# Attention and MLP layer on one core: the maxima's parts and the inverse of the sums move to GpSimd, with one store and two loads of the maxima per tile

## The chip, the cores and the metric

The kernel runs on one core of a Trainium2 chip. Its time is the device time of one execution in microseconds (us), and the time of a kernel is the median of several executions. The engines are named as the profile names them: PE is TensorE's matmul, PEld its weight load, DVE is VectorE, ACT is ScalarE, POOL is GpSimd, and SP is SyncE, which here only issues DMAs. Each engine works through its own instructions in the order in which the program lists them; an instruction that waits holds up all that stand behind it on its engine.

## The reference

The input is one sequence of 2048 rows of 512 numbers. It is normalised, and then goes through two branches whose results are added to the input (S = 2048, D = 512, H = 32 heads of Dh = 16, F = 1792; `q`, `k` and `v` come from `x @ wqkv`):

```python
def _A_ref(x, wqkv, wo):
    ...
    scores = jnp.einsum("bhqd,bhkd->bhqk", q, k) * (Dh ** -0.5)
    p = _softmax(scores, axis=-1)
    o = jnp.einsum("bhqk,bhkd->bhqd", p, v)
    return (lambda x, *d: x.transpose(*d))(o, 0, 2, 1, 3).reshape(B, S, D) @ wo

def _B_ref(x, w1, b1, w2, b2):
    h = jnp.einsum("bsd,df->bsf", x, w1) + b1
    h = _gelu(h)
    return jnp.einsum("bsf,fd->bsd", h, w2) + b2

x = A_x
xn = _layernorm(x, axis=-1)
return x + _A_ref(xn, A_wqkv, A_wo) + _B_ref(xn, B_w1, B_b1, B_w2, B_b2)
```

## The kernel before

**Tiles and units.** The attention is cut into 32 tiles: eight groups of four heads, times four blocks of 512 queries. A tile has 16 units. The function `unit` (from L766) runs once per unit and does two things at once, 19 units apart (`LEAD`). For the tile that is ahead it computes *scores by query*: a product `pS` of 128 queries with 512 keys for each of four heads, of which DVE takes the maximum over the 512 keys (L366, tile `mt`). For the tile 19 units behind it computes *scores by key*: a product `pT` of 128 keys with 512 queries for each of four heads, whose exponential ACT writes to `pe` (L414); the products `pV` of `pe` with the values accumulate over the tile's 16 units. Each product is four matmuls of 32 columns, and works in the upper or the lower 64 rows of PE.

**The filler.** Everything else that PE has to do (projections, both layers of the MLP, the output projection) is cut into products `pD` that `unit` deals out: a group of them has a pace, so that a unit carries 32 or 24 of these matmuls in its two halves (`FAST` and `SLOW`).

**The order inside a unit.** A unit has two halves. In the first it issues `pT`, `pS`, `pS`, `pT` for two of the four heads, and then `pV` and `pD`; in the second the same for the other two heads. Only three PSUM banks hold `pS` (tag S), three hold `pT` (tag T), taken in turn.

**The maxima.** Softmax needs each query's maximum over all keys before the exponential. The maximum, divided by 1024 and negated, is held as two float16 rows (a high part and the rest) in rows 62 and 63 of the operand `qst`, against rows of 1024 in `kst`; the product `pT` then has the maximum subtracted already. So after the last unit of scores of a tile, this chain must be through before `pT` of that tile can start, three units later:

- `s_end` (L375): DVE reduces `mt` to 16 columns of negated maxima, `mneg` (L382), in float32.
- `store` (L385): after the first half of the next unit, PE turns `mneg` with two float32 products against the identity (L390), into a bank of tag T, or of tag S where a group of filler products has just begun (`fresh`).
- DVE writes from that bank the high part (L393) and the rest (L394) into `mhl`.
- SP issues two stores of `mhl` to DRAM (L397) and, when they have landed, four loads into `qst` (L348).

**The sums.** The last column of the values is 1, so `pV` also holds the sums of the exponentials. At the end of a tile (`v_end`, L430) ACT copies `pV` to `osb`; the sums go to DRAM, come back as `dn`, 64x32, DVE inverts them (L458), and they go to DRAM and come back spread over the rows as `rb`. POOL multiplies and splits (L471 to L473). These steps are put into a queue with a delay in units each, 1, 3, 6, 7, 9 and 12 (L483).

**POOL's work** (GELU's products, splits in two float16 parts) is dealt out too: `run_steps` gives out up to `POOL_NS` = 2500 ns of it per unit.

**The start.** The first 19 units of scores, with layernorm and the first projections, are put in order by a planner (`Plan`), which takes the step with the longest chain behind it; `E_TAIL` is the length that it counts behind the first tile's loads of maxima. There the chain of the maxima is written out a second time (L1130 to L1152).

Of the kernel before, what the change touches and what calls it, by code (L numbers as in the profile page):

```python
# [18 lines left out]
P = 128  # L19
# [15 lines left out]
POOL_NS = 2500  # L35
TAIL = 5
WARM = 430
NV = 11
LAG, E_TAIL = 3000, 8000
# [15 lines left out]
def layer_kernel(ctx: ExitStack, tc: tile.TileContext, x, wqkv, wo, w1, b1, w2, b2, out):  # L55
# [19 lines left out]
    m_d = dram.tile([NG * NQB, 16, 2, P], F16, name="m_d")  # L75
# [21 lines left out]
    mnegs = [const.tile([P, 32], F32, name=f"mneg{i}") for i in range(2)]  # L97
    for m in mnegs:
        nc.gpsimd.memset(m, 0.0)
# [244 lines left out]
    def m_rows(t, h):  # L344
        g, qb = divmod(t, NQB)
        p, a = divmod(h, 2)
        dst = qst[g % 2][qb][64 * a + 62:64 * a + 64, p].rearrange("r (t q) -> r t q", q=P)
        nc.sync.dma_start(dst, m_d[t, 4 * h:4 * h + 4].rearrange("t r q -> r t q"))  # L348

    def s_mm(u, n, s):  # L350

        t, i = divmod(u, 16)
        g, qb = divmod(t, NQB)
        qt, kb = divmod(i, 4) if t else (i % 4, i // 4)
        ks, qs = kst[g % 2], qst[g % 2]
        p, a = divmod(n, 2)
        r = slice(64 * a, 64 * a + 62)
        tiled(None, s, qs[qb][r, p, qt * P:(qt + 1) * P], ks[kb][r, p, :], True, True)

    def s_max(u, n, s):  # L360

        t, i = divmod(u, 16)
        qt, kb = divmod(i, 4) if t else (i % 4, i // 4)
        if t not in mt_of:
            mt_of[t] = work.tile([P, 4, 4, 4], F32, name="mt", bufs=2)
        nc.vector.reduce_max(mt_of[t][:, n, qt, kb:kb + 1], s, axis=AX.X)  # L366
        given("dve", 600)
# [7 lines left out]
    def s_end(u):  # L375
# [4 lines left out]
        g, qb = divmod(t, NQB)  # L380
        mneg = mnegs[t % 2]
        nc.vector.tensor_reduce(mneg[:, :16], mt_of[t].rearrange("p h t k -> p (h t) k"), axis=AX.X, op=ALU.max, negate=True)  # L382
        given("dve", 220)

        def store():  # L385
# [3 lines left out]
            for a in range(2):  # L389
                nc.tensor.matmul(pt[32 * a:32 * a + 32, :64], mneg[64 * a:64 * a + 64, :],  # L390
                                 ident[64 * a:64 * a + 64, 64 * a:64 * a + 64], start=True, stop=True)
            mhl = work.tile([64, 2, 64], F16, name="mhl", bufs=2)
            nc.vector.tensor_scalar_mul(mhl[:, 0], pt[:64, :64], 1.0 / MROW)  # L393
            nc.vector.scalar_tensor_tensor(mhl[:, 1], pt[:64, :64], 1.0 / MROW, mhl[:, 0], op0=ALU.mult, op1=ALU.subtract)  # L394
# [35 lines left out]
    def v_end(u):  # L430
# [16 lines left out]
        dn = work.tile([64, 32], F32, name="dn", bufs=1)  # L447
        rb = work.tile([P, QB], F32, name="rb", bufs=1)
# [8 lines left out]
        def inverse():  # L457
            nc.vector.reciprocal(dn, dn)  # L458
            given("dve", 330)
# [23 lines left out]
        at = (1, 3, 6, 7, 9, 12) if t < (NG - 1) * NQB else (1, 2, 5, 6, 7, 8)  # L483
# [282 lines left out]
    def unit(gen):  # L766
# [7 lines left out]
        for a in range(2):  # L774
            for kind, b in ((1, 1), (0, 0), (0, 1), (1, 0)) if a == 0 else ((1, 2), (0, 3), (0, 2), (1, 3)):
# [30 lines left out]
            if a == 0 and u % 16 == 0 and u // 16 - 1 in stores:  # L806
                stores.pop(u // 16 - 1)()
# [12 lines left out]
    with ExitStack() as st1:  # L820
# [309 lines left out]
        def maxima():  # L1130
            nc.vector.tensor_reduce(mnegs[0][:, :16], mt_of[0].rearrange("p h t k -> p (h t) k"), axis=AX.X, op=ALU.max, negate=True)

        a = add("DVE", 220, maxima, m_last)
        mkey = ("S", "m", 0)
        mhl = work.tile([64, 2, 64], F16, name="mhl", bufs=2)

        def turn_m():
            tl[mkey] = sb_tile(mkey)
            for k in range(2):
                nc.tensor.matmul(tl[mkey][32 * k:32 * k + 32, :64], mnegs[0][64 * k:64 * k + 64, :],  # L1140
                                 ident[64 * k:64 * k + 64, 64 * k:64 * k + 64], start=True, stop=True)

        a = add("PE", 300, turn_m, [a], take=[mkey])
        a = add("DVE", 160, lambda: nc.vector.tensor_scalar_mul(mhl[:, 0], tl[mkey][:64, :64], 1.0 / MROW), [a])
        a = add("DVE", 160, lambda: nc.vector.scalar_tensor_tensor(mhl[:, 1], tl[mkey][:64, :64], 1.0 / MROW, mhl[:, 0],
                                                                   op0=ALU.mult, op1=ALU.subtract), [a], free=[mkey])
        put = [add("SP", 600, lambda k=k: nc.sync.dma_start(m_d[0, :, :, 64 * k:64 * k + 64], mhl[32 * k:32 * k + 16]), [a], size=4)
               for k in range(2)]
        for k in range(4):
            def fn(k=k):  # L1150
                m_rows(0, k)
            add("SP", 270, fn, put, size=4, tail=E_TAIL)  # L1152
# [365 lines left out]
```

## Time and profile before

| what | value |
|---|---|
| median of 3 runs | 1451.87 us (1451.73 to 1453.36) |
| the profiled execution's own time | 1450.86 us |
| its span, first to last instruction | 1449.1 us |
| mean granted TensorE clock | 0.996 |
| PE busy | 1432.0 us, 99% of the span |
| DVE busy | 1353.8 us, 93% |
| ACT busy | 1255.9 us, 87% |
| POOL busy | 663.8 us, 46% |
| DMA | 124.86 MB, mean 86 GB/s |

The span is what the profile can account for; 1.8 us of the execution lie around it. Busy time is the union of an engine's instructions: matmuls overlap, so a PE that is always busy can still be late. Rows of a timeline give the start and the length in us, the engine, the line of the kernel, the operation, what it writes and reads, and in brackets the idle time before it with what ended it. Rows of the groups give the count, the busy time of all, the mean in ns of one, and the idle time of the engine just before them. Rows of windows give for each engine the busy time in that stretch, with the number of its instructions.

### The profile page before, as it was taken

Reading aid. Unit: us, or ns where it says so; the run is one execution under the profiler, and the core shown is the slowest. Engines: PE = TensorE matmul, PEld = TensorE weight load, DVE = VectorE, ACT = ScalarE, POOL = GpSimd, SP = SyncE. Lnnn points to the kernel's source line nnn. Section 1 sums busy time; section 2 is a strip of 40 time slices with the busy share of each in tenths; the row PEclk is TensorE's granted clock in tenths of the full one; section 3 lists DMA queues with packets and bytes.
Section 4 is the critical chain, followed back from the end, with each engine's and each line's share of the span. In section 5 each row is a group of like instructions: output and inputs, shape, how many; then the busy total and the mean of one; then the engine's idle time right before and its main releaser. Section 6 shows DMA issues by size and latency. Waiting matters only on the chain.

```text
span 1449.1 us, 88687 instructions
## 1 busy us (share of the span) xinstructions
PE 1432.0 (99%) x40184; PEld 964.6 (67%) x40184; DVE 1353.8 (93%) x2304; ACT 1255.9 (87%) x2367; POOL 663.8 (46%) x673
## 2 busy tenths in 40 slices
PE   8999999999999999999999999999999999999998
PEld 4447767776666767667677766676766767666565
DVE  7989999999999999999999999999999999999933
ACT  5868888888999888899988899998889999888885
POOL 3201857664878401388831138882115787121100
PEclk9999999999999999999999999999999999999999
DMA  7731565455224210221112111121112110111423
GB/s 218 226 122 40 163 202 182 150 181 153 86 64 131 67 34 27 62 70 42 45 44 89 30 37 46 55 74 45 44 39 85 48 38 23 56 55 47 137 65 119
DMA packets 112627, 124.86 MB, mean 86 GB/s; under 512 B 22908, under 2 KB 84220, under 8 KB 112248
## 3 DMA queue, kind: packets, MB, share of 16 engines
q1 hardware_dynamic: 112248, 119.18, 26.8%
q8 instruction: 314, 5.14, 1.5%
q14 instruction: 65, 0.53, 0.1%
HBM read 81.66 MB, written 37.34 MB: 82 GB/s over the span
## 4 chain that ended last, share of the span: by engine, by line
PE 87%; DVE 8%; DMA 2%; ACT 1%; issue 1%; SPq 0%; DVEq 0%; ACTq 0%
PE pD L169 26%; PE pV L169 25%; PE pT L169 17%; PE pS L169 16%; DVE mt L366 7%; PE pT L1015 2%; DMA wq<-in_A_wqkv_dram 1%; PE pD L1015 1%; DMA m_d<-mhl 0%; ACT xs L968 0%; DVE xt L998 0%; ACT pe L414 0%; DMA qst<-m_d 0%; DVE ac L1393 0%; ACT wqk_h L904 0%
## 5 line engine op out<-in xcount | busy, mean ns | idle before, releaser
L366 DVE TENSOR_REDUCE mt<-pS 128x1 f32<-128x512 f32 x2029 | 1277.4, 682 | 34.8 <-PE pS L169 7.8
L414 ACT ACTIVATE pe<-pT 128x512 f32<-128x512 f32 x2048 | 1106.9, 599 | 150.2 <-PE pT L169 65.0
L169 PE MATMUL pV<-pe,vv 64*32 64x512 f32 x8192 | 1087.8, 591 | 0.3 <-issue 0.2
L169 PE MATMUL pT<-qst,kst 64*32 64x512 f16 x8192 | 710.4, 378 | 1.9 <-issue 1.2
L169 PE MATMUL pS<-kst,qst 62*32 62x512 f16 x8116 | 627.0, 378 | 2.6 <-DVE mt L366 2.0
L169 PEld LDWEIGHTS <-qst 62*32 62x32 f16 x8192 | 309.3, 90 | 196.7 <-issue 50.9
L169 PE MATMUL pD<-xb,wc 64*32 64x512 f16 x5376 | 363.9, 375 | 0.0
L169 PE MATMUL pD<-w_s,g 64*32 64x512 f16 x5376 | 361.8, 375 | 0.0
L169 PEld LDWEIGHTS <-kst 64*32 64x32 f16 x8192 | 280.5, 91 | 96.0 <-issue 24.2
L169 PEld LDWEIGHTS pV<-pe,vv 64*32 64x32 f32 x8192 | 245.3, 105 | 13.6 <-PE pV L169 4.2
L169 PEld LDWEIGHTS <-wc 64*32 64x32 f16 x5376 | 160.7, 91 | 44.5 <-issue 0.4
L169 PEld LDWEIGHTS <-g 64*32 64x32 f16 x5376 | 163.5, 91 | 39.2 <-issue 0.5
L169 PE MATMUL pD<-xt,wqk_h 64*32 64x512 f16 x2400 | 159.3, 376 | 0.7 <-issue 0.7
L1360 POOL TENSOR_TENSOR xa<-xa,yt 128x512 f32<-128x512 f32 x16 | 20.5, 1281 | 222.8 <-ACT yt L1358 222.8
L471 POOL TENSOR_TENSOR osb<-osb,rb 128x512 f32<-128x512 f32 x31 | 39.9, 1286 | 159.2 <-DMA rb<-den_d 132.8
L1312 POOL TENSOR_TENSOR t<-hh 128x512 f32<-128x512 f32 x56 | 58.2, 1040 | 77.0 <-ACT hh L1335 75.9
L169 PEld LDWEIGHTS <-wqk_h 64*32 64x32 f16 x2400 | 74.0, 92 | 19.9 <-issue 2.0
L1314 POOL TENSOR_TENSOR t<-t,hh 128x512 f32<-128x512 f32 x56 | 71.8, 1282 | 4.7
L1307 POOL TENSOR_TENSOR t<-t,hh 128x512 f32<-128x512 f32 x56 | 71.7, 1280 | 4.7
L1309 POOL TENSOR_TENSOR g<-t,g 128x512 f16<-128x512 f32 x56 | 65.2, 1164 | 4.7
L1306 POOL TENSOR_SCALAR t<-t,gs 128x512 f32<-128x512 f32 x56 | 38.8, 694 | 54.8 <-ACT t L1301 54.8
L169 PE MATMUL pD<-wo_s,oc 64*32 64x512 f16 x816 | 54.7, 376 | 0.0
(165 smaller groups left out, 895.1 us busy)
## 6 DMA issues: line engine op xcount, KB each, us to landing
wc<-w_d SPq DMA_DIRECT2D x56, 256.0 KB
qk_d<-stg SPq DMA_DIRECT2D x32, 256.0 KB
rb<-den_d SPq DMA_DIRECT2D x124, 64.0 KB
wch<-in_B_w_dram SPq DMA_DIRECT2D x14, 512.0 KB
wch<-in_B_w_dram SPq DMA_DIRECT2D x28, 256.0 KB
w_d<-wsp SPq DMA_DIRECT2D x28, 256.0 KB
kst<-qk_d SPq DMA_DIRECT2D x64, 96.0 KB
qst<-qk_d SPq DMA_DIRECT2D x64, 96.0 KB
```

The source lines that it names most:

```text
L169: p = nc.tensor.matmul(*args, **kw)
L366: nc.vector.reduce_max(mt_of[t][:, n, qt, kb:kb + 1], s, axis=AX.X)
L414: nc.scalar.activation(pe, st, AF.Exp, scale=scale_of[g // 2])
L471: pooled((1280, lambda: nc.gpsimd.tensor_tensor(osb, osb, rb, op=ALU.mult)), (620, lambda: nc.gpsimd.tensor_scalar(ot[:, 0], osb, 1.0, 0.0 ...
L1015: nc.tensor.matmul(tl[key], lhs, rhs, start=c + n == 0, stop=(c, n) == (NC - 1, 2))
L1306: pooled((690, lambda: nc.gpsimd.tensor_scalar(t1, t1, 1.0, gs[:, 1:2], op0=ALU.add, op1=ALU.mult)), (1280, lambda: nc.gpsimd.tensor_tenso ...
L1307: (1280, lambda: nc.gpsimd.tensor_tensor(t1, t1, hh, op=ALU.mult)),
L1309: (1160, lambda: nc.gpsimd.tensor_tensor(g[:, 1, f, :], t1, g[:, 0, f, :], op=ALU.subtract)),
L1312: pooled((1040, lambda: nc.gpsimd.tensor_tensor(t1, hh, hh, op=ALU.mult)), (620, lambda: nc.gpsimd.tensor_scalar(t1, t1, 1.0, 1.0 / GELU_A ...
L1314: (1280, lambda: nc.gpsimd.tensor_tensor(t1, t1, hh, op=ALU.mult)),
L1360: add = lambda: nc.gpsimd.tensor_tensor(xa, xa, yt, op=ALU.add)
```

## The change

What it does:

- DVE still reduces `mt` to 16 columns (now `mx`, not negated). POOL then divides it by 1024, makes the float16 high part, and the float16 rest: three instructions on 128x16 (`m_parts`). DVE's two instructions on the turned maxima are gone.
- PE turns the float16 parts with two products against a float16 matrix of -1 on the diagonal (`m_turn`), and ACT copies the result to `mturned` (`m_copy`). The turning products are issued later: no longer after the first half of the unit, but in the second half, just before its last `pT`.
- `mturned` goes to DRAM in one store, and comes back in two loads. The queries of a block are dealt to the partitions of `pS` in another order (64 from the block's first half, 64 from its second), so that these loads find longer runs; the number of matmuls of `pS` stays.
- The inverse of the sums is four POOL instructions on 64x32: a power with exponent -1, and a Newton step. It is queued with a delay of 5 units (4 for the last group), not 6 (5).
- `POOL_AT`: in the units around the end of a tile `run_steps` gives out 800 ns (before the tile's last unit) and 3100 ns (in the three that follow) of POOL's other work in place of 2500.
- In the start, the planner has the same chain in its new form, and `E_TAIL` is 9500 in place of 8000.

```diff
+POOL_AT = {15: 800, 0: 3100, 1: 3100, 2: 3100}
-LAG, E_TAIL = 3000, 8000
+LAG, E_TAIL = 3000, 9500
-    m_d = dram.tile([NG * NQB, 16, 2, P], F16, name="m_d")
+    m_d = dram.tile([NG * NQB, 2, 2, 2, 8, P // 2], F16, name="m_d")
...
-        room[0] = min(room[0], 0) + POOL_NS
+        room[0] = min(room[0], 0) + (POOL_AT.get(pos[0] % 16, POOL_NS) if pos[0] < NU else POOL_NS)
...
-    def m_rows(t, h):
+    def m_store(t, turned):
+        nc.sync.dma_start(m_d[t].rearrange("s a j r q -> (s a j r) q"), turned)
+
+    def m_rows(t, a):
         g, qb = divmod(t, NQB)
-        p, a = divmod(h, 2)
-        dst = qst[g % 2][qb][64 * a + 62:64 * a + 64, p].rearrange("r (t q) -> r t q", q=P)
-        nc.sync.dma_start(dst, m_d[t, 4 * h:4 * h + 4].rearrange("t r q -> r t q"))
+        dst = qst[g % 2][qb][64 * a + 62:64 * a + 64].rearrange("j p (s n) -> j p s n", s=2)
+        nc.sync.dma_start(dst, m_d[t, :, a].rearrange("s j (p t) q -> j p s (t q)", p=2))
+
+    def m_parts(t):
+        mx = work.tile([P, 2, 8], F32, name="mx", bufs=1)
+        parts = work.tile([P, 2, 2, 8], F16, name="mparts", bufs=2)
+        return (lambda: nc.vector.tensor_reduce(mx.rearrange("p a r -> p (a r)"), mt_of[t].rearrange("p h t k -> p (h t) k"),
+                                                axis=AX.X, op=ALU.max),
+                lambda: nc.gpsimd.tensor_scalar(mx, mx, 1.0 / MROW, 0.0, op0=ALU.mult, op1=ALU.add),
+                lambda: nc.gpsimd.tensor_scalar(parts[:, :, 0], mx, 1.0, 0.0, op0=ALU.mult, op1=ALU.add),
+                lambda: nc.gpsimd.tensor_tensor(parts[:, :, 1], mx, parts[:, :, 0], op=ALU.subtract)), parts
+
+    def m_turn(pt, parts):
+        for s in range(2):
+            nc.tensor.matmul(pt[32 * s:32 * s + 32, :64], parts[64 * s:64 * s + 64].rearrange("p a j r -> p (a j r)"),
+                             nident[64 * s:64 * s + 64], start=True, stop=True)
+
+    def m_copy(pt):
+        turned = work.tile([64, 64], F16, name="mturned", bufs=2)
+        nc.scalar.activation(turned, pt[:64, :64], AF.Copy)
+        return turned
...
-        tiled(None, s, qs[qb][r, p, qt * P:(qt + 1) * P], ks[kb][r, p, :], True, True)
+        for j in range(0, P, 32):
+            c = QB // 2 * (j // 64) + 64 * qt + j % 64
+            product(None, s[j:j + 32], qs[qb][r, p, c:c + 32], ks[kb][r, p, :], start=True, stop=True)
...
-            for a in range(2):
-                nc.tensor.matmul(pt[32 * a:32 * a + 32, :64], mneg[64 * a:64 * a + 64, :],
-                                 ident[64 * a:64 * a + 64, 64 * a:64 * a + 64], start=True, stop=True)
-            mhl = work.tile([64, 2, 64], F16, name="mhl", bufs=2)
-            nc.vector.tensor_scalar_mul(mhl[:, 0], pt[:64, :64], 1.0 / MROW)
-            nc.vector.scalar_tensor_tensor(mhl[:, 1], pt[:64, :64], 1.0 / MROW, mhl[:, 0], op0=ALU.mult, op1=ALU.subtract)
-            given("dve", 300)
-            for a in range(2):
-                nc.sync.dma_start(m_d[t, :, :, 64 * a:64 * a + 64], mhl[32 * a:32 * a + 16])
-            for h in range(4):
-                m_rows(t, h)
+            m_turn(pt, parts)
+            m_store(t, m_copy(pt))
+            for a in (1, 0):
+                m_rows(t, a)
...
         def inverse():
-            nc.vector.reciprocal(dn, dn)
-            given("dve", 330)
+            nc.gpsimd.tensor_tensor(iv, dn, minus1, op=ALU.pow)
+            nc.gpsimd.tensor_tensor(dn, dn, iv, op=ALU.mult)
+            nc.gpsimd.tensor_scalar(dn, dn, -1.0, 2.0, op0=ALU.mult, op1=ALU.add)
+            nc.gpsimd.tensor_tensor(dn, dn, iv, op=ALU.mult)
...
-        at = (1, 3, 6, 7, 9, 12) if t < (NG - 1) * NQB else (1, 2, 5, 6, 7, 8)
+        at = (1, 3, 5, 7, 9, 12) if t < (NG - 1) * NQB else (1, 2, 4, 6, 7, 8)
...
-            for kind, b in ((1, 1), (0, 0), (0, 1), (1, 0)) if a == 0 else ((1, 2), (0, 3), (0, 2), (1, 3)):
+            for i, (kind, b) in enumerate(((1, 1), (0, 0), (0, 1), (1, 0)) if a == 0 else ((1, 2), (0, 3), (0, 2), (1, 3))):
+                if a == 1 and i == 3 and u % 16 == 0 and u // 16 - 1 in stores:
+                    stores.pop(u // 16 - 1)()
...
-            if a == 0 and u % 16 == 0 and u // 16 - 1 in stores:
-                stores.pop(u // 16 - 1)()
```

How this moves instructions is seen best on PE, in the unit that follows a tile's last unit of scores (a tile in the middle of the program, `w_s` and `g` are operands of filler products, `kst` and `qst` the operands of the scores). Before, the turning products stand behind the first half's filler and ahead of the second half's four products of scores:

```order
L169 LDWEIGHTS g
L169 MATMUL pD<-w_s,g 32x512
L390 MATMUL pT<-ident,mneg_100 32x64 x2
L169 LDWEIGHTS kst_3_86
L169 MATMUL pT<-qst_1_92,kst_3_86 32x512
...
L169 LDWEIGHTS qst_3_94
L169 MATMUL pS<-kst_0_83,qst_3_94 32x512
```

Now, in the same unit (`mparts` is what POOL wrote):

```order
L175 LDWEIGHTS g
L175 MATMUL pD<-w_s,g 32x512
L175 LDWEIGHTS kst_3_86
L175 MATMUL pT<-qst_1_92,kst_3_86 32x512
...
L175 LDWEIGHTS qst_3_94
L175 MATMUL pS<-kst_0_83,qst_3_94 32x512
...
L370 LDWEIGHTS mparts
L370 MATMUL pT<-nident,mparts 32x64
...
L175 LDWEIGHTS kst_3_86
L175 MATMUL pT<-qst_1_92,kst_3_86 32x512
```

One `pT` and two `pS` now come ahead of the turning products, and one `pT` behind them.

On POOL, the same kind of place while the MLP's first layer runs: before (`t` and `g` are GELU's tiles, `osb`, `rb` and `ot` the end of the sums' path of the tile before),

```order
L1309 TENSOR_TENSOR g<-t_12832,g 128x512
L1312 TENSOR_TENSOR t_13482<-hh 128x512
L1313 TENSOR_SCALAR t_13482<-t_13482 128x512
L1314 TENSOR_TENSOR t_13482<-t_13482,hh 128x512
L471 TENSOR_TENSOR osb<-osb,rb 128x512
L472 TENSOR_SCALAR ot<-osb 128x512
```

and now:

```order
L1327 TENSOR_TENSOR g<-t_12866,g 128x512
L364 TENSOR_SCALAR mx<-mx 128x16
L365 TENSOR_SCALAR mparts<-mx 128x2x8
L366 TENSOR_TENSOR mparts<-mx,mparts 128x2x8
L1330 TENSOR_TENSOR t_13524<-hh 128x512
L1331 TENSOR_SCALAR t_13524<-t_13524 128x512
L1332 TENSOR_TENSOR t_13524<-t_13524,hh 128x512
L497 TENSOR_TENSOR osb<-osb,rb 128x512
```

The three steps on the maxima stand where POOL's share of a unit has been cut to 800 ns; GELU's next three and the end of the sums' path follow them.

More of the change, by code (lines that the diff above doesn't have):

```diff
@@ L95, in layer_kernel @@
     sexp = const.tile([P, 4], F32, name="sexp")
-    mnegs = [const.tile([P, 32], F32, name=f"mneg{i}") for i in range(2)]
-    for m in mnegs:
-        nc.gpsimd.memset(m, 0.0)
+    nident = const.tile([P, P // 2], F16, name="nident")
+    for a in range(2):
+        nc.gpsimd.tensor_scalar(nident[64 * a:64 * a + 64], ident[64 * a:64 * a + 64, 64 * a:64 * a + 64], -1.0, 0.0,
+                                op0=ALU.mult, op1=ALU.add)
+    minus1 = const.tile([64, 32], F32, name="minus1")
+    nc.gpsimd.memset(minus1, -1.0)
     free_banks = {"S": [0, 1, 2], "T": [3, 4, 5], "D": [6], "V": [7]}
@@ L447, in v_end @@
         dn = work.tile([64, 32], F32, name="dn", bufs=1)
+        iv = work.tile([64, 32], F32, name="iv", bufs=1)
         rb = work.tile([P, QB], F32, name="rb", bufs=1)
@@ L1128, in layer_kernel @@
             score(u)
[L1130 to L1135, printed above, removed]
+        mkey, m_of = ("S", "m", 0), []
+        m_steps, m0 = m_parts(0)
+        a = add("DVE", 220, m_steps[0], m_last)
+        for step in m_steps[1:]:
+            a = add("POOL", 220, step, [a])
         def turn_m():
             tl[mkey] = sb_tile(mkey)
-            for k in range(2):
-                nc.tensor.matmul(tl[mkey][32 * k:32 * k + 32, :64], mnegs[0][64 * k:64 * k + 64, :],
-                                 ident[64 * k:64 * k + 64, 64 * k:64 * k + 64], start=True, stop=True)
+            m_turn(tl[mkey], m0)
         a = add("PE", 300, turn_m, [a], take=[mkey])
[L1144 to L1152, printed above, removed]
+        a = add("ACT", 220, lambda: m_of.append(m_copy(tl[mkey])), [a], free=[mkey])
+        put = add("SP", 420, lambda: m_store(0, m_of[0]), [a], size=4)
+        for k in (1, 0):
+            add("SP", 270, lambda k=k: m_rows(0, k), [put], size=4, tail=E_TAIL)
         for t in range(NV):
```

8 lines of the change are left out of this document (4 added, 4 removed).

## The prediction

> **What bounds the kernel now.** I read the page first: busy shares and the chain that ended last.
>
> ```profile
> span 1449.1 us, 88687 instructions
> PE 1432.0 (99%) x40184; PEld 964.6 (67%) x40184; DVE 1353.8 (93%) x2304; ACT 1255.9 (87%) x2367; POOL 663.8 (46%) x673
> PE 87%; DVE 8%; DMA 2%; ACT 1%; issue 1%; SPq 0%; DVEq 0%; ACTq 0%
> ```
>
> PE carries 87% of the chain, but DVE carries 8%, so the bound changes hands somewhere. The windows tell where. In order: a whole tile whose units carry 32 filler matmuls; one in which units of 32 and 24 alternate; a single unit with 24; one with 32; a unit of 32 with the turning products in it; one of 24 with them; and a stretch of GELU, for POOL.
>
> ```profile
> 1006.22:1048.21 41.99, 41.99 (x1284) 29.49 (x1270) 41.27 (x68) 35.56 (x67) 5.59 (x5) 1.00 0.14 40
> 510.40:551.24 40.84, 40.84 (x1231) 28.80 (x1222) 40.46 (x69) 35.48 (x67) 5.59 (x5) 1.00 0.11 34
> 378.91:381.29 2.38, 2.38 (x81) 1.69 (x73) 2.38 (x4) 2.25 (x6) 2.21 (x3) 1.00 0.55 164
> 1011.07:1013.69 2.62, 2.62 (x91) 1.70 (x80) 2.58 (x5) 2.17 (x5) 0.00 (x0) 1.00 0.04 9
> 1005.67:1008.40 2.73, 2.73 (x97) 2.30 (x84) 2.66 (x7) 2.23 (x5) 0.00 (x0) 1.00 0.03 9
> 1088.89:1091.50 2.61, 2.61 (x85) 1.55 (x69) 2.54 (x8) 2.34 (x5) 0.00 (x0) 1.00 0.02 6
> 675.00:717.00 42.00, 42.00 (x1244) 29.41 (x1232) 41.05 (x70) 39.08 (x75) 34.28 (x37) 1.00 0.18 52
> ```
>
> After each stretch stand its length, then the busy time of PE, PEld, DVE, ACT and POOL. PE alone needs 2.62 us for a unit of 32 and 2.38 for one of 24; sixteen of 32 make 41.9, which is the first tile to 0.1, so **PE sets it**. Eight of each make 40.0, but the second tile takes 40.84. Its other limit is DVE:
>
> ```profile
> L366 DVE TENSOR_REDUCE mt<-pS 128x1 f32<-128x512 f32 x2029 | 1277.4, 682 | 34.8 <-PE pS L169 7.8 <-PE pT L169 6.5 <-PE pV L169 2.3
> L393 DVE TENSOR_SCALAR mhl<-pT 64x64 f16<-64x64 f32 x24 | 5.0, 207 | 0.0
> 1079.76 9.87 DVE mt L366 x16
> ...
> L455 SPq DMA_DIRECT2D dn<-den_d x31: 480/506/1232, 149.5 to 1398.9; - x31
> L458 DVE RECIPROCAL dn<-dn x31: 333/334/336, 160.1 to 1409.3; 64x32 f32<-64x32 f32 x31
> ```
>
> Sixteen maxima in a row take 9.87 us; less one's 0.68, over fifteen, that is 0.613 each, and 39.2 for a tile's 64. What comes on top shows at a tile's end (DVE, a tile that PE sets):
>
> ```profile
> 1006.22 0.22 DVE L382 TENSOR_REDUCE mneg<-mt 128x16 f32<-128x64 f32 x1
> 1006.35 1.28 DVE L366 TENSOR_REDUCE mt<-pS 128x1 f32<-128x512 f32 x2
> 1007.55 0.21 DVE L393 TENSOR_SCALAR mhl<-pT 64x64 f16<-64x64 f32 x1
> 1007.79 0.22 DVE L394 SCALAR_TENSOR_TENSOR mhl<-pT,mhl 64x64 f16<-64x64 f32 x1
> 1007.93 1.87 DVE L366 TENSOR_REDUCE mt<-pS 128x1 f32<-128x512 f32 x3
> ```
>
> L382 costs 0.13 (1006.22 to 1006.35), the two on `mhl` 0.38 (1007.55 to 1007.93), and the reciprocal, of 0.33 and overlapped like the others by some 0.08, 0.25. That makes 40.0, the same as PE's 40.0 in an alternating tile: with three banks between them neither can save up time, and 0.8 us a tile is lost. By their filler, 17 of the 32 tiles are such **tight** tiles.
>
> **The change, part by part.**
>
> *Turning products, later and behind GpSimd: +2.9 us.* I cost this by one number, the time from the start of L382 to the start of the last `pT` of that unit, which now stands behind the turning products. Before:
>
> ```profile
> 1007.32 0.46 PE L169 MATMUL pT<-qst,kst 64*32 64x512 f16 x4
> ...
> 1089.65 0.22 DVE L382 TENSOR_REDUCE mneg<-mt 128x16 f32<-128x64 f32 x1
> 1090.08 0.22 PE L390 MATMUL pT<-ident,mneg 64*32 64x64 f32 x1
> 1090.61 0.40 PE L169 MATMUL pT<-qst,kst 64*32 64x512 f16 x4
> ...
> 922.51 0.22 DVE L382 TENSOR_REDUCE mneg<-mt 128x16 f32<-128x64 f32 x1
> 923.98 0.40 PE L169 MATMUL pS<-kst,qst 62*32 62x512 f16 x4 [0.20 <-DVE mt L366]
> 923.99 0.40 PE L169 MATMUL pT<-qst,kst 64*32 64x512 f16 x4
> ```
>
> It is 1.10 in the first, 0.96 in a tight tile, 1.48 where the turning products took a bank of tag S: there the next `pS` waits for one more maximum. GpSimd's new steps have no row; the nearest are wide ones:
>
> ```profile
> L472 POOL TENSOR_SCALAR ot<-osb 128x512 f16<-128x512 f32 x31 | 19.1, 618 | 2.7
> L473 POOL TENSOR_TENSOR ot<-osb,ot 128x512 f16<-128x512 f32 x31 | 36.1, 1164 | 2.6
> L1218 POOL TENSOR_SCALAR wsp<-wch 128x1024 f16<-128x1024 f32 x14 | 14.6, 1045 | 1.1
> L1219 POOL TENSOR_TENSOR wsp<-wch,wsp 128x1024 f16<-128x1024 f32 x14 | 30.0, 2141 | 1.2
> L99 POOL MEMSET mneg<- 128x32 f32 x2 | 0.2, 131 | 0.0
> ```
>
> From 512 to 1024 columns TENSOR_SCALAR grows by 427 ns and TENSOR_TENSOR by 977, so at 16 columns they cost 191 + 13 = 0.20 us and 187 + 31 = 0.22. The gap between two that depend on each other is 2.7/31 = 0.09. The chain then is 0.22 (L382), a hand-over to POOL, 0.20, 0.09, 0.20, 0.09, 0.22, a hand-over to PE and the product itself. For the two hand-overs I take 0.09, as for that gap, and 0.2: in the tight tile L390 started 0.21 behind the end of L382. With 0.05 for the short float16 product that is **1.36 us** in place of 1.10 and 0.96. POOL is free then. I took the instruction that stands ahead of the three steps in the new order and looked up when it ended in the trace of before; the latest case is this one:
>
> ```profile
> 216.40 1.16 POOL L152 TENSOR_TENSOR wqk_h<-wq,wqk_h 128x512 f16<-128x512 f32 x1
> ...
> 217.83 0.22 DVE L382 TENSOR_REDUCE mneg<-mt 128x16 f32<-128x64 f32 x1
> ```
>
> It ended 0.27 us before L382 began, and in the other tiles 1.1 us or more. The new wait is PE's: behind the turning products stand that unit's last `pT`, then `pV` and the filler, and behind ACT's copy of them one exponential.
>
> What 1.36 costs: the unit with the turning products was 0.11 longer (2.73 against 2.62), and the next 0.06, since `mhl` held DVE up; without them the last `pT` would have come at 1.10 - 0.11 = 0.99. Now it comes 0.37 later than that in place of 0.11 + 0.06: 0.20 worse. The same subtraction, tile by tile from the starts of `pT`, gives +0.12 on average in 15 tiles of the first kind (some lost more than 0.06 in the next unit) and +0.09 in nine of the second (0.23 in its own unit, 2.61 against 2.38, and up to 0.37 in the next). In six tiles with a bank of tag S the turning products now wait for the maximum that `pS` waited for, until 1.48, and `pT` follows at 1.54, +0.05 each. Sum: 1.8 + 0.8 + 0.3 = 2.9 for 30 tiles; the first and the last tile's chains meet other work and count as 0. Bounds: steps as short as L99's 131 ns give 1.14 and -2.4; steps as slow as under the third rival, +15.3.
>
> *DVE's relief: -4.3 us.* That of `mhl` is in the sum above. The reciprocal's 0.25 is worth nothing where PE sets the pace and up to its full size in the 17 tight tiles: 17 x 0.25 = 4.3. Bounds: 0, and 31 x 0.25 = -7.8. I take the tight tiles, since DVE's 40.46 of 40.84 leaves no room there. The four instructions that replace it sit on POOL, which in GELU's stretch is busy 34.28 of 42.00 and elsewhere 5.59 of 41.99. They are queued a unit (2.6 us) earlier; `dn` was fetched 10.6 us ahead of the reciprocal in the first tile (149.5 to 160.1), so it is there. Behind them on SP stands the store of `dn`, two units later.
>
> *Shorter way of the maxima: -1.0 us.* ACT's copy, 0.2 to 0.6 behind its exponentials, comes a little later than DVE's; one store and two loads save three issues of SP. What can be won is what PE lost to late rows:
>
> ```profile
> PEld L169 <- DMA qst<-m_d: 2.8, 5, 0.9
> PE pT L169 <- DMA qst<-m_d: 0.6, 2, 0.3
> ```
>
> Between 0.6 (PE's own) and 3.4 (its weight loads too). The place itself:
>
> ```profile
> 598.13 0.40 PE L169 MATMUL pT<-qst,kst 64*32 64x512 f16 x4
> 599.60 0.40 PE L169 MATMUL pT<-qst,kst 64*32 64x512 f16 x4 [0.31 <-DMA qst<-m_d]
> ```
>
> Here 1.47 us lie between the last `pT` of a unit and the first of the next, where 1007.32 to 1008.40 is 1.08: 0.4 lost. Two more tiles lost 0.5 and 0.15 so; I take 1.0. ACT's copy itself, 31 in all, lies in its idle time (87% busy).
>
> *The start: 0.* The planner orders PE, DVE and SP otherwise, with nearly the same work; up to 1.2 either way, which is the one long wait of PE at its end.
>
> Sum: 2.9 - 4.3 - 1.0 = **-2.4 us**. The profiled execution took 1450.86, 1.0 less than the median of 1451.87; a difference carries over, so I forecast 1449.5, rounded to **1449**.
>
> **The rivals.**
>
> *GpSimd's small steps are nearer to 131 ns.* Then the turn wins 2.4 instead, and the sum is -2.4 - 4.3 - 1.0 = -7.7: **1444**. For it: L99 is the narrowest row. Against it: a memset reads nothing.
>
> *PE sets the pace everywhere.* DVE's relief is worth nothing, and the sum is 2.9 - 1.0: **1454**, no measurable change. For it: PE's 87% of the chain. Against it: the 40.84.
>
> *GpSimd's chain is longer than priced, and PE stands at the turning products (slower).* One place, all 31 tiles. If its steps keep the ratio to DVE's that wide ones have,
>
> ```profile
> L998 DVE TENSOR_TENSOR xt<-pT,xt 128x512 f16<-128x512 f32 x6 | 3.9, 684 | 0.0
> ```
>
> 1164 against 684 is 1.70, and DVE's 0.21 becomes 0.36: the three take 1.07, not 0.62, and the last `pT` starts at 1.8. Then 24 tiles lose 0.45 more, six 0.27, the turn costs 2.9 + 10.8 + 1.6 = 15.3, and the sum is +10.0: **1462**. It decides from 0.1 us more per tile than I priced: 24 x 0.1 = 2.4, and the gain is gone. Against it: the intercepts above, in which both engines' small instructions cost 0.2. The Trainium skill, page "GPSIMD Engine Reference", section 4.1 "Engine selection", says to keep elementwise work on VectorE, with GpSimd about twice as slow for two inputs; the wide rows here agree at 1.70, and no run so far shows a narrow one. By that factor of 2, an estimate, the three steps would take 1.26 us, and the same sum would come to 1468.
>
> *The power is slow, and POOL becomes the bound in GELU's stretch.* There 7.7 us of 42 are free, less 37 gaps of 0.09 and 0.8 for the maxima: 3.6. The inverse's other three steps and gaps take about 1.0, so a power beyond 2.6 us is not covered. Each us more would cost up to 12 us over some twelve such tiles: at 5 us, up to 29, **1478**. Nothing in the trace prices it.
>
> **How the numbers follow.** Chances: the forecast 0.45 (its own range 1446 to 1453), short steps 0.20, PE everywhere 0.13, long chain 0.15, slow power 0.07. No change is what lies within 0.2%, 2.9 us, about what this measurement can tell. Faster: the 0.20, and 0.20 of the forecast's 0.45, since 1449 is just at that bound: 0.40. Slower: 0.22, and 0.03 of the others: 0.25. Same: 0.35. The range for 8 in 10 reaches from 1442, below the short steps' case, to 1460, just short of the long chain's.
>
> **What would show it.** Right: in the profile of the changed kernel POOL's first two steps on `mx` and `mparts` take about 0.20 and the third 0.22, the last `pT` of that unit starts 1.3 to 1.4 behind DVE's reduction, and PE's waits name POOL there; tight tiles get shorter by 0.15 on average, and a tile like the first above rises from 41.99 to about 42.2; PE waits no more for `m_d`. Wrong: if the three steps together take under 0.5 or over 0.8, or if tight tiles do not get shorter; if ACT's tanh or PE wait for POOL during GELU, the power decides.

## The result, and the profile after

The changed kernel takes 1468.6 us (median; 1468.35 to 1469.68) beside 1452.23 for the kernel before: a ratio of 1.0115 [1.0102, 1.0128], 16.4 us slower. The forecast was 1449, 0.2% faster, with a range from 1442 to 1460. The profiled execution took 1468.35.

The page of the changed kernel (its span, busy time, and the chain that ended last):

```profile
span 1466.6 us, 88632 instructions
PE 1435.5 (98%) x40120; PEld 961.8 (66%) x40120; DVE 1348.0 (92%) x2209; ACT 1261.6 (86%) x2399; POOL 874.8 (60%) x894
PE 72%; POOL 17%; DVE 4%; issue 2%; DMA 2%; ACT 1%; SPq 1%; POOLq 0%; DVEq 0%; ACTq 0%
```

PE has 3.5 us more busy time than before, and the span 17.5. POOL, which was not in the chain of the kernel before at all, has 17% of it. Its busy time rose from 663.8 to 874.8, by 211. The groups of its new instructions (count, busy time and mean ns, idle time before them and its releaser) say where from:

```profile
L482 POOL TENSOR_TENSOR iv<-dn,minus 64x32 f32<-64x32 f32 x31 | 168.4, 5433 | 87.4 <-DMA dn<-den_d 87.3
...
L366 POOL TENSOR_TENSOR mparts<-mx,mparts 128x16 f16<-128x16 f32 x32 | 7.0, 219 | 2.7
L364 POOL TENSOR_SCALAR mx<-mx 128x16 f32<-128x16 f32 x32 | 6.6, 206 | 189.0 <-DVE mx L362 189.0
L365 POOL TENSOR_SCALAR mparts<-mx 128x16 f16<-128x16 f32 x32 | 6.5, 205 | 2.6
```

One power takes 5.43 us, sixteen times DVE's reciprocal of 0.33, and makes 168 of the 211. The steps on the maxima took what they were priced at.

The waits (engine and line, what was waited for: us in total, times, longest) name the place, and the late rows of `m_d` no longer stand among PE's longer ones (0.7 us in all, beside 2.8 and 0.6 before):

```profile
PEld L370 <- POOL mparts L366: 18.3, 28, 5.0
PE pT L370 <- POOL mparts L366: 9.8, 5, 4.7
ACT t L1319 <- POOL t L1332: 3.5, 2, 2.6
PE pT L175 <- ACT pe L437: 2.5, 2, 2.1
```

PE waits at the turning products (L370) for POOL: up to 4.7 us at once. Most tiles are not like that. This is one on time, in the timeline, from DVE's reduction (L362) to the last `pT`:

```profile
564.14 0.22 DVE L362 TENSOR_REDUCE mx<-mt 128x16 f32<-128x64 f32 x1
564.45 0.20 POOL L364 TENSOR_SCALAR mx<-mx 128x16 f32<-128x16 f32 x1 [12.68 <-DVE mx L362]
564.73 0.21 POOL L365 TENSOR_SCALAR mparts<-mx 128x16 f16<-128x16 f32 x1
565.02 0.22 POOL L366 TENSOR_TENSOR mparts<-mx,mparts 128x16 f16<-128x16 f32 x1
565.29 0.20 PE L370 MATMUL pT<-nident,mparts 64*32 64x64 f16 x2
565.30 0.40 PE L175 MATMUL pT<-qst,kst 64*32 64x512 f16 x3
```

POOL had been idle for 12.68 us; the parts were ready 1.10 behind the start of the reduction, the last `pT` started at 1.16. Twenty tiles look like this (1.16 to 1.28), and five more, with a bank of tag S, had it at 1.47 to 1.54. In six tiles, counted from the first as 0, POOL was not idle, and the last `pT` came at 5.98 (tile 2), 2.65 (8), 1.94 (9), 3.13 (14), 2.52 (20) and 2.98 (21). The worst, on POOL and then PE:

```profile
162.67 5.45 POOL L482 TENSOR_TENSOR iv<-dn,minus 64x32 f32<-64x32 f32 x1
168.21 0.25 POOL L483 TENSOR_TENSOR dn<-dn,iv 64x32 f32<-64x32 f32 x1
...
169.06 0.61 POOL L652 TENSOR_SCALAR stg<-pf 128x512 f16<-128x512 f32 x1
...
176.51 0.22 DVE L362 TENSOR_REDUCE mx<-mt 128x16 f32<-128x64 f32 x1
...
179.55 2.12 POOL L1237 TENSOR_TENSOR wsp<-wch,wsp 128x1024 f16<-128x1024 f32 x1
181.63 0.20 POOL L364 TENSOR_SCALAR mx<-mx 128x16 f32<-128x16 f32 x1
...
182.48 0.24 PE L370 MATMUL pT<-nident,mparts 64*32 64x64 f16 x2 [4.68 <-POOL mparts L366]
```

From the power to L364 POOL works without a gap of more than 0.1 us: 19 us of work, of which the inverse is 6.4 (162.67 to 169.06). The reduction was done at 176.73, and its parts stood in POOL's queue for 4.9 us. In the other five late tiles, too, POOL works from the power to L364 without a gap of more than 0.2 us, for 17.3 to 18.7 us.

With the start of each unit (its first `pT`) taken from both traces, the span's 17.5 us divide so:

| where | us |
|---|---|
| up to the first unit with `pT` (93.18 to 95.18) | +2.0 |
| the three units around the turning products, in the six late tiles | +14.1 |
| the same, in the other 25 tiles | -0.8 |
| one unit during GELU, 1221.09 to 1227.69, before 2.62 long | +4.0 |
| all other units | -1.8 |

The unit during GELU has the power in the chain of waits, asked for that stretch (start, length, what):

```profile
1215.03 5.44 POOL iv L482
...
1221.41 1.23 POOL t L1332
...
1222.66 0.03 ACT t L1319
1222.69 0.51 issue
1223.20 0.59 ACT pe L437
```

ACT's tanh waits for the GELU step behind the power, and an exponential stands behind the tanh. The last row of the table is for the most part no effect of the change: two units in it, of -1.36 and -1.37, are shorter by nearly as much (1.37 and 1.30) in the kernel with three reciprocals (below), which has no part of the change. The +0.9 that is left is spread over many units and the program's end, and its cause was not looked for.

### The profile page after: what moved, and what is told of

It is laid out like the page before. It is cut to its first block, busy times and chain, and to the rows that moved or that the text cites. A ratio compares the mean times of both kernels' runs of the same rounds, so it can differ in the third digit from the quotient of the medians.

```text
span 1466.6 us, 88632 instructions
## 1 busy us (share of the span) xinstructions
PE 1435.5 (98%) x40120; PEld 961.8 (66%) x40120; DVE 1348.0 (92%) x2209; ACT 1261.6 (86%) x2399; POOL 874.8 (60%) x894
## 4 chain that ended last, share of the span: by engine, by line
PE 72%; POOL 17%; DVE 4%; issue 2%; DMA 2%; ACT 1%; SPq 1%; POOLq 0%; DVEq 0%; ACTq 0%
PE pD L175 21%; PE pV L175 20%; PE pT L175 14%; PE pS L175 13%; DVE mt L396 3%; POOL iv L482 3%; POOL t L1325 2%; PE pT L1041 2%; POOL t L1332 2%; POOL g L1327 2%; POOL t L1330 2%; POOL t L1324 1%; POOL t L1331 1%; POOL g L1326 1%; ACT pe L437 1%
## 5 line engine op out<-in xcount | busy, mean ns | idle before, releaser
L175 PEld LDWEIGHTS pV<-pe,vv 64*32 64x32 f32 x8192 | 241.2, 105 | 13.1 <-PE pV L175 4.1
L482 POOL TENSOR_TENSOR iv<-dn,minus 64x32 f32<-64x32 f32 x31 | 168.4, 5433 | 87.4 <-DMA dn<-den_d 87.3
L364 POOL TENSOR_SCALAR mx<-mx 128x16 f32<-128x16 f32 x32 | 6.6, 206 | 189.0 <-DVE mx L362 189.0
```

Of the source, the lines that this page charges most:

```text
L175: p = nc.tensor.matmul(*args, **kw)
L482: nc.gpsimd.tensor_tensor(iv, dn, minus1, op=ALU.pow)
```

## Which half costs: the inverse, the parts, or both together

After the result my theory was: the power's 5.4 us make POOL late, and the parts of the maxima make PE wait behind POOL, so that neither half alone costs what both do. A rival was that the later and longer way of the maxima costs by itself; another, that the slow power alone binds POOL.

**The inverse back on DVE**, the rest of the change kept:

```diff
-            nc.gpsimd.tensor_tensor(iv, dn, minus1, op=ALU.pow)
-            nc.gpsimd.tensor_tensor(dn, dn, iv, op=ALU.mult)
-            nc.gpsimd.tensor_scalar(dn, dn, -1.0, 2.0, op0=ALU.mult, op1=ALU.add)
-            nc.gpsimd.tensor_tensor(dn, dn, iv, op=ALU.mult)
+            nc.vector.reciprocal(dn, dn)
+            given("dve", 330)
```

> The changed kernel with the inverse of the sums back on DVE (one reciprocal, at the new delay of 5 units); the maxima's path stays as changed. Theory 'long power': the power's 5.43 us makes POOL late at the tile's end, and PE stands at the turning products for it; without it the six late tiles (13.5 us together) and the wait of 4.2 us in one GELU tile are gone, the last pT starts 1.16 us behind the reduction in every tile without a bank of tag S, and the time is 1451 to 1455. DVE gets 31 x 0.25 us back, which costs nothing. Rival 'place': it is the maxima's way over POOL as such that costs; the time stays above 1462.

Measured: 1451.12 us, ratio 0.9986 [0.9974, 0.9997]. PE's wait at the turning products is gone but for the weight load's 0.2 a tile:

```profile
PEld L370 <- POOL mparts L366: 4.7, 23, 0.6
```

Without the power the 16 us are gone, and no tile is late: the last `pT` is at 1.15 to 1.20 in all 25 tiles without a bank of tag S.

**The power alone**, in the kernel before: the maxima's way is the old one (with one tile `mneg` in place of two, which makes room for `iv`).

```diff
-            nc.vector.reciprocal(dn, dn)
-            given("dve", 330)
+            nc.gpsimd.tensor_tensor(iv, dn, minus1, op=ALU.pow)
+            nc.gpsimd.tensor_tensor(dn, dn, iv, op=ALU.mult)
+            nc.gpsimd.tensor_scalar(dn, dn, -1.0, 2.0, op0=ALU.mult, op1=ALU.add)
+            nc.gpsimd.tensor_tensor(dn, dn, iv, op=ALU.mult)
...
-        at = (1, 3, 6, 7, 9, 12) if t < (NG - 1) * NQB else (1, 2, 5, 6, 7, 8)
+        at = (1, 3, 5, 7, 9, 12) if t < (NG - 1) * NQB else (1, 2, 4, 6, 7, 8)
```

> The kernel before with the four POOL instructions for the inverse alone (power and Newton step, delay of 5 units); the maxima stay on DVE, and no PE instruction waits for POOL at a tile's end. Theory 'long power': POOL is as late as in the changed kernel, but nobody stands behind it there: 1452 to 1458, the rest being ACT's tanh where it waits for POOL. Rival 'POOL is the bound in GELU's stretch whatever waits for it': 1463 or more. Rival 'DVE's relief is worth 4 us': 1448.

Measured: 1452.95 us, ratio 1.0002 [0.9992, 1.0012]. The group of the power:

```profile
L461 POOL TENSOR_TENSOR iv<-dn,minus 64x32 f32<-64x32 f32 x31 | 168.4, 5432 | 92.7 <-DMA dn<-den_d 92.6
```

Once the start is over, the longest wait of PE's weight loads for POOL is that of a filler product for GELU's result:

```profile
PEld L171 <- POOL g L1314: 1.5, 1, 1.5
```

And POOL's queue in the timeline, at the place of the worst tile:

```profile
161.47 5.45 POOL L461 TENSOR_TENSOR iv<-dn,minus 64x32 f32<-64x32 f32 x1
...
178.30 2.15 POOL L1224 TENSOR_TENSOR wsp<-wch,wsp 128x1024 f16<-128x1024 f32 x1
```

The same 168 us of power, and POOL just as late (it works on `wsp` at the same distance from the power as above), cost nothing that the median shows, since no one at the tile's end stands behind POOL. So a power of 5.4 us does not bind POOL by itself, and the halves, free or nearly so alone, cost 1.15% together: the theory holds and both rivals fall. DVE's reciprocal is gone here, too, and the units that held it are as long as before (0.00 us at the median): a first sign that DVE's relief is worth nothing.

**A subtraction in the power's place** (`dn` less `dn`, the rest of the four instructions kept, so the inverse itself is left out). The power's instruction also waits for `dn` at the head of POOL's queue, 87 us in all; this keeps the wait and takes away the length.

```diff
-            nc.gpsimd.tensor_tensor(iv, dn, minus1, op=ALU.pow)
+            nc.gpsimd.tensor_tensor(iv, dn, dn, op=ALU.subtract)
```

> The changed kernel with a subtraction of the same shape in place of the power: four POOL instructions, the same waits, the same order; the inverse of the sums is left out of the computation. Theory 'long power': only the duration matters, 1451 to 1455 as with the reciprocal on DVE. Rival 'waits at the head of the queue': POOL waited 87 us in all for the DMA that brings dn, with GELU's work standing behind; if that or the number of instructions makes POOL late, the time stays above 1462.

The group of the subtraction:

```profile
L482 POOL TENSOR_TENSOR iv<-dn 64x32 f32<-64x32 f32 x31 | 7.2, 233 | 86.2 <-DMA dn<-den_d 86.1
```

Its wait at the turning products:

```profile
PEld L370 <- POOL mparts L366: 4.9, 24, 0.6
```

Measured: 1453.21 us, ratio 1.0006 [0.9996, 1.0016]. The wait for `dn` is the same, and no tile is late through POOL (in tile 2 the last `pT` came at 1.59, but POOL had been idle for 0.92 us before its steps). It is the length. DVE has no reciprocal here either, and in the first of these experiments it has one: 1.0006 beside 0.9986, so the relief brought no gain.

**The power on 128x16** in place of 64x32: the same 2048 numbers, half the columns.

```diff
-    minus1 = const.tile([64, 32], F32, name="minus1")
+    minus1 = const.tile([P, 16], F32, name="minus1")
...
-        dn = work.tile([64, 32], F32, name="dn", bufs=1)
-        iv = work.tile([64, 32], F32, name="iv", bufs=1)
+        dn = work.tile([P, 16], F32, name="dn", bufs=1)
+        iv = work.tile([P, 16], F32, name="iv", bufs=1)
...
```

> The changed kernel with the sums laid out as 128 partitions x 16 columns in place of 64 x 32, the same 2048 numbers. If the power is paid per column, it takes 2.7 us and the time falls to 1453 to 1458; if per number or per instruction, it stays at 5.4 us and 1468.

The group of the power:

```profile
L482 POOL TENSOR_TENSOR iv<-dn,minus 128x16 f32<-128x16 f32 x31 | 90.3, 2914 | 83.8 <-DMA dn<-den_d 83.7
```

The waits at the turning products:

```profile
PEld L370 <- POOL mparts L366: 8.3, 26, 2.2
PE pT L370 <- POOL mparts L366: 1.9, 1, 1.9
```

Measured: 1455.3 us, ratio 1.0030 [1.0014, 1.0045]. With 2.91 us a power two tiles are late (3.18 in tile 2, and 2.05 in one more) and cost 4.6 us together, and the unit during GELU is 2.62 long again; with 0.23 none is, with 5.43 six are, at 14.1. The cost follows the length, but it is not in proportion to it: what counts is whether POOL has caught up by the tile's end.

**POOL's list told of the power.** `run_steps` deals out POOL's other work by a budget that does not count the inverse. Here 2500 ns are taken off when the inverse is issued:

```diff
+            room[0] -= 2500
             nc.gpsimd.tensor_tensor(iv, dn, minus1, op=ALU.pow)
```

> The change with the power on POOL, but the list of POOL's other steps is told of it: 2500 ns of the budget are taken off when the inverse is queued, so one unit's steps are put off. Theory that the six late tiles come from POOL's queue standing 3 to 6 us behind where the list puts it, because the list does not count the power: the lateness falls by up to 2.5 us a tile, from 5.98, 2.65, 1.94, 3.13, 2.52, 2.98 to about 3.5 in one tile and the plain 1.16 in the others, 8 to 10 us less: 1458 to 1461. Rival, that POOL simply has more work there than a tile has time, and the steps put off come back later in the same tiles: no gain, 1466 to 1470, or ACT's tanh waits for POOL instead and the time is higher.

PE's waits for POOL:

```profile
PE pT L370 <- POOL mparts L366: 10.4, 4, 4.7
...
PE pD L175 <- POOL g L1328: 2.2, 1, 2.2
```

Measured: 1475.01 us, ratio 1.0151 [1.0134, 1.0168]. My expectation fell: tiles 8 and 21 came on time, but 9, 20 and 27 came later than in the changed kernel (3.78, 4.01 and 2.87), and tile 2 stayed at 5.95. A filler product now also waits for GELU's result `g`. Work that is put off by a unit comes back ahead of another reduction: in tile 27 the reduction had ended at 1238.90, and GELU's steps kept POOL until 1240.70. So the missing entry in the budget is not the cause by itself; whether any order of POOL's work would hide the power was not tried. With 5700 ns taken off, about the power's whole length, there is no time: in that order the kernel's engines wait for each other in a circle (a deadlock).

## What DVE's relief is worth

**Three reciprocals in place of one**, in the kernel before. The three, one behind the other, take 1.09 us where one takes 0.33.

```diff
-            nc.vector.reciprocal(dn, dn)
+            for _ in range(3):
+                nc.vector.reciprocal(dn, dn)
```

> The kernel before with three reciprocals one behind the other on DVE in place of one (the inverse of the inverse of the inverse): two more of 0.33, some 0.5 to 0.6 us of DVE a tile. Theory of the prediction, that DVE sets the 17 tiles with units of 32 and 24 in turn: 17 x 0.5 to 0.6 = 8.5 to 10 us more, 1461 to 1463, and those tiles' spans grow by 0.5 each. Theory after the result, that DVE's work at this place does not set them (0.64 us less of it a tile changed them by under 0.03): under 2 us more, 1452 to 1455.

Measured: 1470.57 us, ratio 1.0134 [1.0117, 1.0151], 19 us more, against both expectations. The unit of the reciprocal, in the same tight tile (units of 32 and 24 in turn), by windows (length, then busy time of PE, PEld, DVE, ACT and POOL): of the kernel before, with one reciprocal;

```profile
538.00:540.39 2.39, 2.39 (x81) 1.73 (x73) 2.39 (x5) 2.01 (x5) 0.00 (x0) 1.00 0.02 3
```

of the changed kernel, with none;

```profile
550.86:553.24 2.38, 2.38 (x80) 1.72 (x72) 2.36 (x4) 2.00 (x5) 0.91 (x1) 1.00 0.31 114
```

and of the kernel with three:

```profile
545.71:548.77 3.06, 2.62 (x80) 1.43 (x72) 2.99 (x7) 2.37 (x5) 0.00 (x0) 1.00 0.02 3
```

The timeline of that kernel shows what happens in it:

```profile
546.20 1.09 DVE L459 RECIPROCAL dn<-dn 64x32 f32<-64x32 f32 x3
547.21 2.41 DVE L366 TENSOR_REDUCE mt<-pS 128x1 f32<-128x512 f32 x4
547.88 0.40 PE L169 MATMUL pS<-kst,qst 62*32 62x512 f16 x4 [0.44 <-DVE mt L366]
```

None: 2.38. One: 2.39. Three: 3.06, because `pS` waits for a bank that the late maximum still holds. A unit with 24 takes 2.38 by PE alone, so one reciprocal was already hidden to 0.01, and there was nothing to win; but nearly nothing was left under it either. The next maximum begins 1.01 behind the first reciprocal's start (546.20 to 547.21), in place of the 0.25 that the prediction gives one reciprocal; these 0.76 more cost 0.67 in the unit. It is not only so in tight tiles: in 29 tiles one unit is 0.46 to 0.76 longer. DVE is a bound only from one side here: relief at this place is worth nothing, and a load of 0.76 us costs most of itself.

Relief of DVE did pay in another unit, the one behind the turning products, where DVE was busy without a gap. This is that unit in a tight tile, before, with the two instructions on `mhl` ahead of it, and in the changed kernel, without them:

```profile
553.28:555.83 2.55, 2.55 (x80) 1.46 (x72) 2.55 (x5) 1.95 (x5) 0.00 (x0) 1.00 0.03 3
566.39:568.77 2.38, 2.38 (x77) 1.59 (x72) 2.22 (x4) 1.73 (x4) 1.95 (x3) 1.00 0.06 10
```

The prediction has this gain inside its term for the turning products, not under DVE's relief.

## The later place, the start, and a shorter chain

**The turning products at their old place**, ahead of the second half's products, with the inverse on DVE:

```diff
-                if a == 1 and i == 3 and u % 16 == 0 and u // 16 - 1 in stores:
-                    stores.pop(u // 16 - 1)()
...
+            if a == 0 and u % 16 == 0 and u // 16 - 1 in stores:
+                stores.pop(u // 16 - 1)()
```

> The change with the inverse as DVE's reciprocal (1451.12), but the turning products at their old place on PE, at the end of the unit's first half, ahead of the second half's products. Theory that PE must then stand until POOL has the parts (1.10 behind the start of DVE's reduction; the turning products of the kernel before started 0.43 behind it): 0.5 to 0.65 us in each of the some 25 tiles without a bank of tag S, and the same in the six others, since the products stood at 0.43 there too or waited for a maximum until 1.48; PE can win back nothing of it, as it sets these units: 10 to 18 us more, 1461 to 1469. Rival, that the hold-up is only passed from PE to DVE's banks, which stand ahead by a maximum or two: under 4 us more, 1451 to 1455.

Measured: 1458.7 us, ratio 1.0042 [1.0027, 1.0056], between the two expectations; with the later place it was 0.9986. POOL's last step and the products in its timeline:

```profile
557.79 0.22 POOL L366 TENSOR_TENSOR mparts<-mx,mparts 128x16 f16<-128x16 f32 x1
558.06 0.20 PE L370 MATMUL pT<-nident,mparts 64*32 64x64 f16 x2 [0.41 <-POOL mparts L366]
```

PE stands, as the theory has it, but half as dear: the unit with the products takes 3.33 us in this tile, 0.51 more than in the kernel before (2.82) but only 0.24 more than with the later place (3.09). I had taken the whole stall as extra, although the later place already pays half of it. The 25 tiles without a bank of tag S lose 5.2 us by it in the unit with the products, of the 7.6 between the two medians; the rest was not traced.

**`E_TAIL` at 8000 again**, with the inverse on DVE (`LAG, E_TAIL = 3000, 8000` for `3000, 9500`):

> The change with the inverse as DVE's reciprocal, and E_TAIL put back from 9500 to 8000, so that the start is planned nearer to before. The same with E_TAIL 9500 measured 1451.12. If the start's planning of the change costs something (the first unit came 1.4 to 3.0 us later in the kernels run so far): 1448 to 1450, with the first unit back by 1 to 2 us. If the start's differences are only those between one execution and the next: 1451 +-1, no change.

Measured: 1451.35 us, ratio 1.0003 [0.9992, 1.0013]. The first unit with `pT` starts at 95.79 (96.22 with 9500, and 95.85 in the kernel with the old place): no effect that can be told. In the kernels here it starts between 93.18 (before) and 96.30, and with three reciprocals and with the power alone, whose start is that of the kernel before, at 94.34 and 94.56. So over a us of the changed kernel's 2.0 can be the difference between two executions; what is left could not be told apart.

**Two steps on POOL, not three**: the factor 1/1024 goes into the matrix of the turning products. The inverse is on DVE, and `E_TAIL` is 8000.

```diff
-        nc.gpsimd.tensor_scalar(nident[64 * a:64 * a + 64], ident[64 * a:64 * a + 64, 64 * a:64 * a + 64], -1.0, 0.0,
+        nc.gpsimd.tensor_scalar(nident[64 * a:64 * a + 64], ident[64 * a:64 * a + 64, 64 * a:64 * a + 64], -1.0 / MROW, 0.0,
...
-                lambda: nc.gpsimd.tensor_scalar(mx, mx, 1.0 / MROW, 0.0, op0=ALU.mult, op1=ALU.add),
```

> As the kernel with DVE's reciprocal and E_TAIL 8000, but the factor 1/1024 of the maxima is put into the small matrix that the turning products multiply by, so POOL has two steps between DVE's reduction and PE, not three. Theory that PE stands at the turning products for the chain of POOL's steps (parts ready 1.10 behind the reduction, last pT at 1.16): both come 0.22 + 0.08 = 0.30 earlier, parts at 0.80; in the some 24 tiles without a bank of tag S PE gains up to 0.2 to 0.3 each, 5 to 7 us, so 1445 to 1447. Rival, that the last pT cannot come earlier than some 1.0 because DVE's maxima of the unit hold its banks (0.96 to 1.10 in the kernel before): 0.1 a tile, 1449 to 1451.

The tile that was shown on time above, in this kernel's timeline:

```profile
551.85 0.22 DVE L362 TENSOR_REDUCE mx<-mt 128x16 f32<-128x64 f32 x1
552.24 0.21 POOL L364 TENSOR_SCALAR mparts<-mx 128x16 f16<-128x16 f32 x1 [19.11 <-DVE mx L362]
552.53 0.22 POOL L365 TENSOR_TENSOR mparts<-mx,mparts 128x16 f16<-128x16 f32 x1
...
552.80 0.41 PE L175 MATMUL pT<-qst,kst 64*32 64x512 f16 x4
```

And PE's wait for the parts:

```profile
PEld L369 <- POOL mparts L365: 0.7, 2, 0.4
```

Measured: 1446.95 us, ratio 0.9970 [0.9959, 0.9981]: faster than both kernels. The parts were ready at 0.90, not 0.80 (POOL's first step began 0.39 behind the reduction, not 0.31; why was not looked for), and the last `pT` came at 0.95 here and 1.04 in tiles of 32. By then PE waits for POOL in two tiles only, so the chain is shorter than what PE does anyway, and the rival's bound holds: 3.1 us gained over the 25 tiles without a bank of tag S, 0.12 each and not 0.2 to 0.3. The rest of the 4.4 us between the two medians matches an earlier start in the profiled executions (94.20 against 95.79). So the time lies in the theory's range, 1445 to 1447, while the gain per tile is the rival's; with the start of the other kernel it would lie near the rival's 1449.

## Why the prediction was wrong

| term | forecast | measured |
|---|---|---|
| turning products | +2.9 | about +0.6 in the 25 tiles on time; +0.9 in all 31 without the power |
| DVE's relief | -4.3 | 0 |
| shorter way of the maxima | -1.0 | about -1.0; another -0.3 that kernels without the change show too |
| start | 0, up to 1.2 either way | +2.0, part of it between executions |
| power on POOL | 0 | +14.1 at the turning products of the six late tiles (0.3 to 0.5 there without the power), +4.0 in GELU |

**The step that failed first** is "POOL is free then". It was looked up from the instruction ahead of the three steps in the trace of before, in which POOL does not have the power. The change puts 31 x 6.4 us of inverse into the same queue, some six units ahead of the reduction, and POOL's other work stands behind it. The look-up gave the right answer for a POOL without the power: with the subtraction or DVE's reciprocal no tile is late through POOL. The power's own cost had no row and got no bounds in the sum. It was a rival with a chance of 0.07, whose tipping point of 2.6 us turned out to be half of the price.

**That rival had the cause and not the mechanism.** It looked for POOL as the bound in GELU's stretch, where ACT's tanh would wait, in about twelve tiles, 12 us for each us of power. There the power cost one unit, 4.0 us, and without the new way of the maxima that unit is 0.3 longer, and the median is that of the kernel before. The loss came through the wait that the other half of the change made: PE's wait for POOL at the turning products, whose price I had worked out for a POOL that is there at once. The rival of the longer chain had the place right (PE stands at the turning products) and the reason wrong, a price per step: six tiles lost 0.8 to 6.8 us each in place of all of them a little.

**DVE's relief** failed as a step too. The sum of PE's own times and of DVE's, 40.0 each over a tight tile, was no proof that DVE sets it. Unit by unit, in the tile whose reciprocal is shown above, 0.37 of its 0.83 us over 40.0 stand in the unit with the turning products and the next (2.82 and 2.55, where PE needs 2.62 and 2.38), 0.25 and 0.09 in two others, and 0.01 in the reciprocal's. The 0.25 and the 0.09 are there in the changed kernel, too; what sets those two units was not looked for. That the reciprocal's unit had nothing to give could be read in the trace of before. The tight tile shown in the prediction went from 40.84 to 40.85 (of the changed kernel, as is the tile of 32 below):

```profile
523.29:564.14 40.85, 40.85 (x1230) 28.70 (x1222) 40.27 (x66) 35.61 (x68) 12.31 (x12) 1.00 0.12 35
1021.87:1063.92 42.05, 42.05 (x1275) 29.25 (x1266) 41.03 (x66) 35.67 (x68) 13.52 (x13) 1.00 0.13 39
```

The rival that PE sets the pace everywhere was right that DVE's relief is worth nothing. Its sum, 2.9 - 1.0 = +1.9, a ratio of 1.0013, lies within the interval of the kernel with the subtraction (1.0006) and outside that of the one with DVE's reciprocal (0.9986). That PE sets every unit was not shown.

**The turning products** were right as a mechanism. The steps took 0.21, 0.21 and 0.22 (0.20, 0.20 and 0.22 were priced), the hand-over to POOL 0.09 as priced, that to PE 0.05 (565.24 to 565.29) in place of 0.2, and the `pT` behind the product started 0.01 later, not 0.05, so that the last `pT` came at 1.16 and not 1.36; with a bank of tag S 1.47 to 1.54 (1.54 forecast). The rule of the Trainium skill, page "GPSIMD Engine Reference", section 4.1 "Engine selection", by which GpSimd is about twice as slow for two inputs, does not come out at 16 columns: POOL's subtraction took 219 ns, and DVE's operations on two tensors of 128x4 in the kernel before (L959, L960 and L963) 156 to 162, so the ratio is at most 1.4 if 16 columns take DVE no less than 4. That the prediction's estimate by this rule, 1468, is the measured time is chance: it doubles all three steps, two of which have one input, to 1.26 us, and they took 0.63. The tile of 32 that was to rise to about 42.2 rose to 42.05.

**The way of the maxima**: the three places named, of 0.4, 0.5 and 0.15, gained 0.62, 0.53 and 0.20. The 0.20, and 0.14 of the 0.62, are gained in the kernel with three reciprocals as well, which has the old way, so they belong to that execution of the kernel before: about 1.0 is left, as forecast.

## What to carry to other kernels

An operation without a row in the trace needs bounds in the sum, not only a rival, and its time has to be written into its engine's queue before anyone asks whether that engine is free: two halves of a change that are free alone can meet in one queue. Judge relief on an engine in the unit in which it stands, not by its share over a stage; the bound at the reciprocal took most of a loss and paid no gain.

## What the hardware showed

- The power on POOL took 5.43 us on 64x32 and 2.91 on 128x16, the same 2048 numbers. If the partitions cost nothing, that is 2.52 us for 16 columns, with 0.4 besides; there are these two shapes alone. The multiplications of the same tiles took 0.25 and 0.22.
- POOL's float16 rest on 128x16 cost what DVE's did on 64x64 (0.22), and PE's product started 0.05 behind the end of POOL's last step.
